# One joint key maximum for the first batch, an order of use for its loads, and weight splitting queued behind its attention on VectorE

## The chip, the cores and the metric

The kernel runs on one core of a Trainium2 chip. The metric is the time of one execution on the device in microseconds (us). The core's engines work in order, each on its own queue: PE multiplies matrices (PEld is its loading of weights), DVE is VectorE, ACT is ScalarE, POOL is GpSimd, and SP here only issues DMAs. They wait for one another through semaphores.

## The reference

Everything is float32; there are 8 batches, 8 heads, 576 rows and 64 columns per head (512 columns together).

```python
q_s = softmax(q, axis=-1)            # over the 64 columns of a row
k_s = softmax(k, axis=2)             # over the 576 rows: one maximum per column of k
kv  = einsum('bhsd,bhse->bhde', k_s, v)
x   = einsum('bhsd,bhde->bhse', q_s, kv)        # heads side by side: 576 x 512
xk, xr = mu_k*x + (1-mu_k)*x_prev, mu_r*x + (1-mu_r)*x_prev   # x_prev: one row earlier
y   = sigmoid(xr @ w_r) * (relu(xk @ w_k)**2 @ w_v)           # 512->512, 512->1024->512
u   = y + real(fft(fft(y, axis=1), axis=2))
out = u + relu(layernorm(u) @ w_ch1) @ w_ch2                  # 512->2048->512
```

q, k, v come in float32; the weight matrices come in 64 bits per element and are turned into float32 on the chip, by `split64`.

## The kernel before

There are three stages: attention with the first pair of matrix layers (until about 690 us), the transform, and the last pair of layers. The change is in the first stage, at its start.

**Attention of one batch n.** Work on k and v goes by head pairs hp = 0 to 3: `k_load` fetches a pair of heads of k and of v, `k_max` takes the maximum over five row blocks in VectorE, `k_col` transposes the 128x128 rest on TensorE (L188), takes one maximum per column (`kc`) and puts it on a diagonal (`kd`); `k_sub` multiplies the diagonal by a matrix of ones (L198), which spreads the maxima over all partitions, and subtracts them from k (L200); `k_exp` is ScalarE's exponential; `k_kv` multiplies with v in ten matrix instructions (L221); `k_out` divides and splits the product in a high and a low part (`kvh` by ScalarE, `kvl` by VectorE, L237). Work on q goes by three row groups T, B and L: `q_load`, `q_max`, `q_sub`, `q_exp`, `q_sum`, `q_mul` (GpSimd), `q_tr` (transposes, L330, and a split). `q_x` multiplies both and leaves x in `xb` (ScalarE's copies, L354 to L361).

**The matrix layers** go by blocks c = 0 to 11 of 384 rows; block 0 needs batch 0, block 1 needs batches 0 and 1, block 2 batch 1. `mix_diff` and `mix_part` make xk and xr (VectorE, with a high part by ScalarE and a low part by GpSimd), `m_wk` is xk @ w_k in eight slices f (L438 to L440), `m_r` is xr @ w_r, `m_wv` the product with w_v (L469 to L471).

**Weights.** Twenty pieces of 128x512 (eight of w_k, four of w_r, eight of w_v) go through five buffers `raw`. A piece is loaded by SP (L62), scaled by ScalarE (L67, L71), put together by VectorE in two steps (L72, L75), rounded to its high part by ScalarE (L81) and given a low part by GpSimd (L82), after which its buffer is free. The high and low parts of w_v lie where batch 0's attention and block 0's mixing had buffers (`spare`).

**What sets the order.** The framework plans the whole program at build and puts the instructions of each engine in a fixed order: the earliest in the text goes first among those that its own estimate has ready. So a later piece of text fills gaps of an earlier one. Buffers of one name (tag) are given out in the order of the text; PE's order in the trace is that of the `pa` tiles in the text. Attention's small matrix products and transposes share the four PSUM buffers `pa`, the column maxima `km` have two buffers, a k tile (`kt`) two, and q's exponentials (`qe`) one. Two waits are written by hand (`after`): the first five weight loads wait for the last load of batch 0 (`early[0]`), and all k and q loads of batch 1 wait for the high part of weight piece 5 (`early[1]`, L81). SP issues batch 0's loads as k pair 0, q T, B, L, then k pairs 1 to 3; GpSimd's queue issues v of pairs 0 and 1.

## Time and profile before

| | us |
|---|---|
| median of three runs (lowest, highest) | 1672.36 (1671.45, 1673.94) |
| the profiled execution | 1676.39 |
| its span, first to last instruction | 1674.6 |
| PE busy | 1548.0 (92%) |
| DVE, ACT, POOL busy | 746.7, 594.9, 491.5 |

The profile is of one execution. Its page gives each engine's busy time and cuts the span into 40 slices of 41.9 us; the views below list instructions in order of time, sums over stretches, and groups of equal instructions.

### The profile page before, as it was taken

The page shows a single profiled execution, that of the slowest core. Times are in us where ns is not written, and L with a number is a line of the kernel's source. Part 1 is how long each engine was busy: PE and PEld are TensorE (multiplying, and loading weights), DVE is VectorE, ACT ScalarE, POOL GpSimd, SP SyncE. Part 2 cuts the span into 40 slices and gives each one's busy share as a digit, 9 for nine tenths or more (in the row PEclk, how much of TensorE's full clock was granted, in tenths as well). Part 3 has the DMA queues.
Part 4 walks back from the last instruction along what each step waited for, and adds up shares of the span by engine and source line. Part 5 has one row for each costly group of instructions (what it writes and reads, how often), then busy time and mean ns, then how long its engine had stood idle before and what let it go on. Part 6 is the DMA issues. An engine that isn't in the chain of part 4 may idle for free.

```text
span 1674.6 us, 19835 instructions
## 1 busy us (share of the span) xinstructions
PE 1548.0 (92%) x7560; PEld 1313.2 (78%) x7560; DVE 746.7 (45%) x1342; ACT 594.9 (36%) x1120; POOL 491.5 (29%) x532
## 2 busy tenths in 40 slices
PE   2497999899989999987887999999999999999998
PEld 2476899788879888776765888888888888888886
DVE  7966544645365442199999312212221313131211
ACT  4673666566556564233445111111111111111110
POOL 4464663646365555265445000000000000000000
PEclk9598999999999999988999999999999999999999
DMA  7521322222212101435454101001010101010000
GB/s 196 164 83 51 85 56 68 64 56 70 69 51 63 58 13 51 170 110 196 167 192 157 51 0 41 11 1 50 1 51 1 50 1 51 0 51 1 26 0 26
DMA packets 117863, 108.91 MB, mean 65 GB/s; under 512 B 54760, under 2 KB 91752, under 8 KB 117512
## 3 DMA queue, kind: packets, MB, share of 16 engines
q1 hardware_dynamic: 107736, 84.37, 17.1%
q10 hardware_dynamic: 8064, 14.68, 2.4%
q0 software_dynamic: 1968, 8.60, 1.4%
q8 instruction: 59, 0.97, 0.2%
q14 instruction: 36, 0.29, 0.1%
HBM read 79.31 MB, written 28.31 MB: 64 GB/s over the span
## 4 chain that ended last, share of the span: by engine, by line
PE 66%; DVE 12%; issue 10%; POOL 4%; ACT 4%; DMA 3%; SPq 1%; POOLq 0%; ACTq 0%; DVEq 0%
PE ph L853 6%; PE ph L855 6%; PE pc L900 6%; PE ph L854 6%; PE pc L902 6%; PE pc L901 6%; PE pv L469 3%; PE pv L470 3%; PE pv L471 3%; PE pk L438 3%; PE pk L439 3%; PE pk L440 3%; DVE xm L416 2%; PE pr L454 1%; PE pr L455 1%
## 5 line engine op out<-in xcount | busy, mean ns | idle before, releaser
L859 DVE SCALAR_TENSOR_TENSOR hl<-ph,hh 128x512 fp32r<-128x512 f32 x144 | 99.2, 689 | 443.8 <-ACT hh L858 443.8
L858 ACT ACTIVATE hh<-ph 128x512 fp32r<-128x512 f32 x144 | 85.9, 597 | 515.3 <-PE ph L855 515.3
L884 POOL DMA_INDIRECT out_dram<-ua,rev x16 | 15.7, 979 | 732.0 <-DVE ua L905 731.6
L902 PE MATMUL pc<-w2h,hl 128*128 128x512 f32 x576 | 222.9, 393 | 8.2 <-DVE hl L859 8.2
L900 PE MATMUL pc<-w2h,hh 128*128 128x512 f32 x576 | 226.5, 393 | 3.9 <-ACT hh L858 3.9
L901 PE MATMUL pc<-w2l,hh 128*128 128x512 f32 x576 | 224.8, 390 | 0.0
L416 DVE SCALAR_TENSOR_TENSOR xm<-dt,omu,xb 128x63 f32<-128x63 f32 (+4 forms) x224 | 115.7, 566 | 83.2 <-POOL xr_lo L425 35.0
L438 PE MATMUL pk<-xk_hi,wk_hi 128*128 128x384 f32 x384 | 131.0, 350 | 12.4 <-ACT xk_hi L424 11.4
L446 POOL TENSOR_TENSOR kk_lo<-h,kk_hi 128x384 fp32r<-128x384 f32 x96 | 98.8, 1033 | 148.6 <-ACT h L445 130.7
L902 PEld LDWEIGHTS pc<-w2h,hl 128*128 128x128 f32 x576 | 107.6, 188 | 35.3 <-DVE hl L859 11.6
L439 PE MATMUL pk<-xk_lo,wk_hi 128*128 128x384 f32 x384 | 131.4, 343 | 0.2 <-POOL xk_lo L425 0.2
L900 PEld LDWEIGHTS pc<-w2h,hh 128*128 128x128 f32 x576 | 108.1, 188 | 29.9 <-ACT hh L858 6.5
L853 PE MATMUL ph<-uha,w1h 128*128 128x512 f32 x320 | 127.7, 401 | 2.8 <-ACT w1h L81 2.8
L440 PE MATMUL pk<-xk_hi,wk_lo 128*128 128x384 f32 x384 | 130.1, 340 | 0.0
L855 PE MATMUL ph<-uha,w1l 128*128 128x512 f32 x320 | 127.3, 398 | 1.2 <-POOL w1l L82 1.2
L854 PE MATMUL ph<-ula,w1h 128*128 128x512 f32 x320 | 126.8, 396 | 0.0
L901 PEld LDWEIGHTS pc<-w2l,hh 128*128 128x128 f32 x576 | 108.2, 188 | 23.6
L469 PE MATMUL pv<-wv,kk_hi 128*128 128x512 f32 x288 | 113.1, 394 | 0.6 <-ACT sgt L458 0.6
L470 PE MATMUL pv<-wv,kk_hi 128*128 128x512 f32 x288 | 112.9, 394 | 0.0
L471 PE MATMUL pv<-wv,kk_lo 128*128 128x512 f32 x288 | 112.4, 393 | 0.0
L853 PE MATMUL ph<-uhb,w1h 128*128 128x512 f32 x256 | 100.9, 397 | 0.0
L855 PE MATMUL ph<-uhb,w1l 128*128 128x512 f32 x256 | 100.0, 391 | 0.0
(206 smaller groups left out, 3178.6 us busy)
## 6 DMA issues: line engine op xcount, KB each, us to landing
raw<-in_moe_w_ch_dram SPq DMA_DIRECT2D x32, 512.0 KB
x1d<-sgt ACTq DMA_DIRECT2D x36, 256.0 KB
ua<-ud SPq DMA_DIRECT2D x36, 256.0 KB
kt<-in_k_dram SPq DMA_DIRECT2D x32, 256.0 KB
xtt<-x1d SPq DMA_DIRECT2D x8, 1024.0 KB
vt<-in_v_dram SPq DMA_DIRECT2D x60, 128.0 KB
qtT<-in_q_dram SPq DMA_DIRECT2D x8, 512.0 KB
qtB<-in_q_dram SPq DMA_DIRECT2D x8, 512.0 KB
```

Of the source, the lines that this page charges most:

```text
L438: nc.tensor.matmul(pk, wh, xk_hi[:, kt], start=kt == 0, stop=False)
L439: nc.tensor.matmul(pk, wh, xk_lo[:, kt], start=False, stop=False)
L440: mm = nc.tensor.matmul(pk, wl, xk_hi[:, kt], start=False, stop=kt == NK - 1)
L469: nc.tensor.matmul(pv, kk_hi[f][:, ts], wv_hi[f // 2][:, f % 2], start=f == 0, stop=False)
L470: nc.tensor.matmul(pv, kk_hi[f][:, ts], wv_lo[f // 2][:, f % 2], start=False, stop=False)
L471: mm = nc.tensor.matmul(pv, kk_lo[f][:, ts], wv_hi[f // 2][:, f % 2], start=False, stop=f == NF1 - 1)
L853: nc.tensor.matmul(ph_, w1h[f][:, kt], uh[:, kt], start=kt == 0, stop=False)
L854: nc.tensor.matmul(ph_, w1h[f][:, kt], ul[:, kt], start=False, stop=False)
L855: nc.tensor.matmul(ph_, w1l[f][:, kt], uh[:, kt], start=False, stop=kt == NK - 1)
L900: nc.tensor.matmul(a, hh[:, cs], w2h[f], start=f == 0, stop=False)
L901: nc.tensor.matmul(a, hh[:, cs], w2l[f], start=False, stop=False)
L902: nc.tensor.matmul(a, hl[:, cs], w2h[f], start=False, stop=f == NF2 - 1)
```

## The change

Batch 0's key work is regrouped. All four `k_load` are issued with one `q_load` after each of the pairs 1, 2 and 3; then all four `k_max`; then q group T's first steps; then one `k_cols`, which transposes the four maxima into one PSUM tile, takes all column maxima in one instruction, builds one diagonal tile of 128x512 and spreads it with one matrix product. The per-pair steps `k_shift`, `k_kv`, `k_out` follow, with q's steps between them. For the weights, the first of VectorE's two steps of each piece (`sign`, L72 of before) is ordered behind the last `kvl` and the last `q_tr` subtraction of batch 0; the order is one on VectorE's queue alone, with no semaphore. The second step depends on the first. The new diagonal tile takes 2 KB of a partition, and GpSimd's memory for DMA descriptors is set to 4096 bytes.

```diff
@@ -57,11 +57,16 @@
             ins.ins, to, mybir.DependencyInfo(mybir.DependencyClass.Sync, mybir.DependencyReason.DATA), reason="pace"
         )

+    def behind(ins, to):
+        tc.add_manual_dep(
+            ins.ins, to, mybir.DependencyInfo(mybir.DependencyClass.NoSync, mybir.DependencyReason.DATA), reason="order"
+        )
+
     def raw64(pool, dst, src, n, bufs, eng):
         raw = pool.tile([P, 2 * n], I32, tag="raw", name="raw", bufs=bufs)
         return raw, eng.dma_start(dst(raw), src)

-    def split64(raw, hi, lo, low_on_dve=False):
+    def split64(raw, hi, lo, low_on_dve=False, late=()):
         low, high = raw[:, 0::2], raw[:, 1::2]
         scaled = high.bitcast(F32)
         nc.scalar.activation(out=scaled, in_=scaled, func=AF.Copy, scale=2.0**-112)
@@ -69,9 +74,11 @@
             nc.vector.tensor_scalar(low, low, 29, None, op0=ALU.logical_shift_right)
         else:
             nc.scalar.activation(out=low, in_=low.bitcast(U32), func=AF.Copy, scale=LOW_SCALE, bias=LOW_BIAS)
-        nc.vector.scalar_tensor_tensor(
+        sign = nc.vector.scalar_tensor_tensor(
             out=low, in0=high, scalar=-(2**31), in1=low, op0=ALU.bitwise_and, op1=ALU.bitwise_or
         )
+        for to in late:
+            behind(sign, to)
         nc.vector.scalar_tensor_tensor(
             out=low, in0=high, scalar=3, in1=low, op0=ALU.logical_shift_left, op1=ALU.bitwise_or
         )
@@ -192,11 +199,33 @@
             nc.vector.tensor_scalar(kd, ident, kc, None, op0=ALU.mult)
             state["kd", n, hp] = (kd, pm)

+
+        def k_cols(pool):
+            pm, bm = (ps.tile([P, NHP, P], F32, tag="pa", name=f"p{i}m0", bufs=4) for i in "mb")
+            for hp in range(NHP):
+                nc.tensor.transpose(pm[:, hp], state.pop(("km", 0, hp)), ident)
+            kc = pool.tile([P, NHP], F32, name="kc4")
+            nc.vector.tensor_reduce(out=kc, in_=pm, axis=AX.X, op=ALU.max)
+            kd = pool.tile([P, NHP, P], F32, name="kd4")
+            nc.vector.tensor_tensor(
+                out=kd,
+                in0=ident.unsqueeze(1).to_broadcast([P, NHP, P]),
+                in1=kc.unsqueeze(2).to_broadcast([P, NHP, P]),
+                op=ALU.mult,
+            )
+            nc.tensor.matmul(bm.rearrange("p h n -> p (h n)"), ones, kd.rearrange("p h n -> p (h n)"), start=True, stop=True)
+            for hp in range(NHP):
+                state["bm", hp] = bm[:, hp]
+
         def k_sub(n, hp):
             kt = state["k", n, hp]
-            kd, pm = state.pop(("kd", n, hp))
-            nc.tensor.matmul(pm[:, P : 2 * P], ones, kd, start=True, stop=True)
-            ka = pm[:, P : 2 * P].rearrange("p (h d) -> p h d", h=2)
+            if n == 0:
+                ka = state.pop(("bm", hp))
+            else:
+                kd, pm = state.pop(("kd", n, hp))
+                ka = pm[:, P : 2 * P]
+                nc.tensor.matmul(ka, ones, kd, start=True, stop=True)
+            ka = ka.rearrange("p (h d) -> p h d", h=2)
             nc.vector.tensor_tensor(
                 out=kt, in0=kt, in1=ka.unsqueeze(2).to_broadcast([P, 2, 5, DH]), op=ALU.subtract
             )
@@ -234,7 +263,7 @@
                 )
             for h in range(2):
                 r = slice(h * DH, (h + 1) * DH)
-                nc.vector.scalar_tensor_tensor(
+                ins = nc.vector.scalar_tensor_tensor(
                     out=kvl[0][r, hp, r],
                     in0=pk[r, r],
                     scalar=rs[r],
@@ -242,6 +271,8 @@
                     op0=ALU.mult,
                     op1=ALU.subtract,
                 )
+                if n == 0:
+                    last["k"] = ins.ins.name

         def q_load(n, g):
             if g == "L":
@@ -336,7 +367,9 @@
                     cs = slice(j, w, 2) if g == "T" else slice(w - 1 - j, None, -2)
                     o = (qh[:, :, cs], ql[:, :, cs], qh.bitcast(F32)[:, :, cs])
                 nc.scalar.copy(o[0], ptv)
-                nc.vector.tensor_tensor(out=o[1], in0=ptv, in1=o[2], op=ALU.subtract)
+                ins = nc.vector.tensor_tensor(out=o[1], in0=ptv, in1=o[2], op=ALU.subtract)
+                if n == 0:
+                    last["q"] = ins.ins.name
             state["qT", n, g] = (qh, ql, w)

         def q_x(n, g):
@@ -363,6 +396,8 @@

         done = set()

+        last = {}
+
         KST = [k_load, None, k_max, k_col, k_shift, k_kv, k_out]
         QST = [q_load, None, None, q_max, q_sub, q_exp, q_sum, q_mul, q_tr, q_x]

@@ -490,7 +525,7 @@
             if src is w_v:
                 hi, lo, i = hi[i // 2], lo[i // 2], i % 2
             at = (slice(None), slice(None), cs) if by_col else (slice(None), i)
-            return split64(raw, hi[at], lo[at])
+            return split64(raw, hi[at], lo[at], late=last.values())

         NRAW = 5
         pieces = [(w_k, wk_hi, wk_lo, f, True) for f in range(NF1)]
@@ -530,13 +565,22 @@

         with tc.tile_pool(name="wst", bufs=1) as wst:
             for hp in range(NHP):
-                for i, fn in enumerate((k_load, k_max, k_col, k_shift, k_kv, k_out)):
+                k_load(0, hp)
+                if hp:
+                    q_load(0, "TBL"[hp - 1])
+            for hp in range(NHP):
+                k_max(0, hp)
+            for fn in (q_max, q_sub, q_exp):
+                fn(0, "T")
+            k_cols(wst)
+            for hp in range(NHP):
+                for fn in (k_shift, k_kv, k_out):
                     fn(0, hp)
-                    if i == 0 and hp == 0:
-                        for g in "TBL":
-                            q_load(0, g)
+                if hp < 2:
+                    for fn in (q_max, q_sub, q_exp):
+                        fn(0, "BL"[hp])
                 if hp < 3:
-                    for fn in (q_max, q_sub, q_exp, q_sum, q_mul, q_tr):
+                    for fn in (q_sum, q_mul, q_tr):
                         fn(0, "TBL"[hp])
             for g in "LTB":
                 q_x(0, g)
@@ -975,7 +1019,7 @@
     from concourse import mybir as _mybir
     from concourse.bass_utils import run_bass_kernel_spmd as _run

-    nc = _bacc.Bacc("TRN2", target_bir_lowering=False, num_devices=1)
+    nc = _bacc.Bacc("TRN2", target_bir_lowering=False, num_devices=1, dynamic_dma_scratch_size=4096)
     arrays, args = {}, []
     tab_s, tab_d = _tables()
     for name, a in [(n, inputs[n]) for n in _INS] + [("tab_s", tab_s), ("tab_d", tab_d)]:
```

## Rows read from the trace of the kernel before

**Rows 1.** The page's forty slices of the span: PE's busy tenths.
```profile
PE   2497999899989999987887999999999999999998
```

**Rows 2.** Windows of the start: length; PE, PEld, DVE, ACT, POOL busy (count); PE clock.
```profile
0.00:20.00 20.00, 3.78 (x13) 2.92 (x13) 12.67 (x29) 4.67 (x5) 6.07 (x16) 1.00 0.78 179
20.00:43.00 23.00, 7.03 (x30) 6.10 (x30) 21.47 (x33) 14.27 (x28) 12.59 (x8) 0.96 0.72 215
43.00:73.00 30.00, 15.62 (x63) 13.52 (x63) 29.08 (x47) 21.77 (x40) 9.96 (x7) 0.50 0.72 218
73.00:96.00 23.00, 16.00 (x75) 14.65 (x76) 19.20 (x33) 13.65 (x31) 17.73 (x19) 0.73 0.32 94
96.00:126.00 30.00, 26.79 (x139) 22.90 (x138) 16.23 (x29) 22.48 (x39) 14.70 (x13) 1.00 0.17 43
126.00:154.00 28.00, 21.15 (x109) 18.40 (x108) 13.42 (x29) 8.14 (x19) 8.50 (x13) 0.76 0.17 51
```

**Rows 3.** Instructions in order of time on PE: start, length, line [idle before].
```profile
25.89 0.42 PE L188 MATMUL pm<-ident,km 128*128 128x128 f32 x1
...
73.64 0.41 PE L188 MATMUL pm<-ident,km 128*128 128x128 f32 x1
80.18 1.01 PE L438 MATMUL pk<-xk_hi,wk_hi 128*128 128x384 f32 x2 [6.12 <-ACT xk_hi L424]
...
127.24 1.28 PE L221 MATMUL pkv<-vt,ek 128*128 128x130 f32 x10
...
136.04 0.39 PE L471 MATMUL pv<-wv,kk_lo 128*128 128x512 f32 x1
```

**Rows 4.** Instructions in order of time on ACT, first 170 us.
```profile
42.93 0.66 ACT L81 CAST wk_hi<-raw 128x512 fp32r<-128x512 f32 x1 [1.06 <-DVE raw L75]
...
154.09 0.59 ACT L359 COPY xb<-pxB 128x512 f32<-128x512 f32 x1 [0.29 <-PE pxB L352]
```

**Rows 5.** Instructions in order of time on DVE, first 90 us.
```profile
22.91 0.58 DVE L237 SCALAR_TENSOR_TENSOR kvl<-pkv,rs,kvh 64x64 fp32r<-64x64 f32 x2 [0.51 <-ACT kvh L232]
...
28.37 0.69 DVE L72 SCALAR_TENSOR_TENSOR raw<-raw 128x512 int32<-128x512 int32 x1
...
36.00 1.79 DVE L72 SCALAR_TENSOR_TENSOR raw<-raw 128x512 int32<-128x512 int32 x1
...
89.17 1.35 DVE L179 TENSOR_REDUCE km<-kt 128x128 f32<-128x640 f32 x1
```

**Rows 6.** Windows again, of the weights' `raw` tiles alone: DVE, ACT, POOL.
```profile
43.00:73.00 30.00, 15.72 (x18) 17.48 (x29) 9.96 (x7) 0.50 0.72 218
...
sum 180.00, DVE 37.26 ACT 36.42 POOL 29.97; mean DVE 5.32 ACT 5.20 POOL 4.28
```

**Rows 7.** DMA issues on SP in order of time.
```profile
84.11 0.39 SPq L158 DMA_DIRECT2D kt<-in_k_dram  x1
```

**Rows 8.** The chain that ended last, at its start.
```profile
5.03 9.40 DMA ql<-in_q_dram
```

**Rows 9.** Groups of DVE and PE in the first 80 us: count, busy us, mean ns.
```profile
L200 DVE TENSOR_TENSOR kt<-kt,pm 128x640 f32<-128x640 f32 x4 | 3.2, 812 | 0.0
L264 DVE TENSOR_REDUCE qmL<-ql 64x8 f32<-64x512 f32 x2 | 1.3, 674 | 0.4 <-DMA ql<-in_q_dram 0.4
L221 PE MATMUL pkv<-vt,ek 128*128 128x130 f32 x40 | 10.1, 440 | 14.9 <-ACT ek L207 14.9
L198 PE MATMUL pm<-kd,ones 128*128 128x128 f32 x8 | 3.2, 502 | 13.6 <-DVE kd L192 8.0 <-DMA raw<-in_moe_w_k_dram 5.6
L330 PE MATMUL ptT<-ident,qeT 128*128 128x128 f32 x8 | 2.0, 428 | 6.5 <-POOL qeT L303 6.5
```

**Rows 10.** Instructions in order of time on POOL.
```profile
35.86 6.49 POOL L82 TENSOR_TENSOR wk_lo<-raw,wk_hi 128x512 fp32r<-128x512 f32 x4 [2.14 <-ACT wk_hi L81]
...
107.59 1.31 POOL L82 TENSOR_TENSOR wv<-raw,wv 128x512 fp32r<-128x512 f32 x1 [1.84 <-ACT wv L81]
```

**Rows 11.** DMA issues by line over the whole span: size, us to landing.
```profile
vt<-in_v_dram POOLq DMA_DIRECT2D x4, 128.0 KB, 7.5
```

## The prediction

> **What bounds the kernel now.** I read the page's slices first. PE is busy nearly throughout, except in the first two slices of 41.9 us (2 and 4 tenths) and the fourth (7 tenths) [rows 1]. A change in batch 0 can only be worth what PE idles there. The windows of the start come next [rows 2]: between 20 and 73 us DVE is busy 50.6 of 53 us while PE has 22.7 of 53, at the lower of its two clock levels (granted 0.50, 1.2 GHz) from 43 on. From 96 us on DVE is no longer full (16.2 of 30), PE is (26.8 of 30); then comes a second hole, 126 to 154 us, where PE has 21.2 of 28 us and DVE, ACT and POOL are all below half. So there are two different limits: VectorE first, then a chain of waits.
>
> The time view of PE shows the chain's stations [rows 3]. Head pair 1 of batch 0 starts its column transpose at 25.89; batch 0's q_x ends and batch 1's first transpose (L188) follows at 73.64; block 0's first m_wk starts at 80.18 and its last m_wv ends at 136.43; batch 1's last k_kv starts at 127.24; ScalarE's last copy of batch 1's x ends at 154.09 + 0.59 = 154.7 [rows 4]. Block 1 needs that copy. PE's second hole is the wait for batch 1, and its chain, 73.64 to 154.7 = 81.0 us, starts where batch 0 ends. That is the number that matters: **what the change is worth is how much earlier batch 1's x is complete**, not how much earlier block 0 starts.
>
> **The change part by part.** *Loads.* The 3.54 MB of q, k and v (three times 8 x 576 x 64 x 4 bytes) at 179 GB/s [rows 2] take 19.8 us in either order. With k pair 3 and its v in front of q L only, its k lands at about 18.5 us. The L load took 9.4 us and the chain ran through it [rows 8]; at the end of the list nothing but the weights' loads stands behind it. If it takes as long there, these start at about 31 us instead of right behind the rest, and five of them (0.52 MB each) at 179 GB/s are in by 46, the first by 34; cover: VectorE takes the first up at about 42 (below) and needs over 1 us for each. Without that cover it would cost the difference, up to 9 us.
>
> *Joint maximum.* Before, the pairs went one after another: four times transpose, kc, kd, L198, k_sub. Now: last k_max to 19.8 us, transposes to 20.2; then two operations of 128x512 that the trace does not have. For the reduction and the diagonal I take 0.68 us each, from the 64x512 reduction [rows 9] (bounds: 0.3, not better than the same work on a quarter; 1.4, all lanes twice as slow); 21.6 us. The product with ones over 512 columns lies between 0.8 us, what the two passes over 128 columns took in all (3.2 / 4) [rows 9], and four times that, 3.2; I take 2.2, since columns and not the start make up most of it; 23.8. The first k_sub 0.81 [rows 9] and an exponential of about the same length: the first k_kv at 25.4. Four of them take 10.1 us and the three transposes of q lying between them 2.0 + 2.0 + about 1 [rows 9] (the last two bounded by the first): 40.5. k_out's parts are near 0.6 each (two instructions 0.58) [rows 5], with a ScalarE part of that kind ahead of them: 42 us, with 38 and 48 as bounds. The rest of q_x, three of each twelve products, about 3 us: 45, against 73.6. Block 0's first m_wk follows q_x by 80.18 - 73.64 = 6.5 us: 51.5 instead of 80.2.
>
> *Weights behind attention.* VectorE's two steps now cannot begin before 42 us; they began at 28.37 [rows 5]. Nothing is saved: in all the weights hold VectorE 37.3 us in this stage [rows 6], and they move as a block from beside batch 0 to beside block 0's mixing and batch 1. What queues behind: ScalarE's L81, then GpSimd's L82, and since the five buffers are freed by L82 only, SP stands at the sixth weight load, with batch 1's loads behind it. And batch 1's loads wait by hand for piece 5's L81. In the trace that came at 42.93 + 0.66 = 43.6, 15.2 us after the first L72. Now five pieces lie scaled in their buffers when VectorE comes, so the way from first L72 to piece 5's L81 is between one piece's round (two steps of 0.69, L81 0.66, L82 1.3, a load of 0.52 MB / 179 GB/s = 2.9, scaling by two ScalarE instructions at about 36.4 / 60 = 0.6 [rows 6], two steps and L81 again: 9.5) and 15.2; I take 12.5: 54.5. **This is the step that goes the wrong way**: batch 1's loads come 11 us later than before. From SP's issue to the end of k_max were 89.17 + 1.35 - 84.11 = 6.4 us for a later pair [rows 5, 7], so batch 1's first transpose comes at 61, not at 73.64: 12.6 us earlier. Before, its k had lain ready and waited for q_x.
>
> *Batch 1's chain.* I keep its 81 us: 142 instead of 154.7. Bounds: its four head pairs took 127.24 - 73.64 = 53.6 us, 13 per pair; the links beside a free PE could be some 3 us shorter each (down to 69 us in all), and some 12 longer if weights lie in its way.
>
> *Is anything else late by then?* Block 0 took 136.4 - 80.2 = 56.3 us on PE; from 51.5 it would end at 108, and its second half needs w_v, whose last low part ended at 107.59 + 1.31 = 108.9 [rows 10], 27.5 us before block 0's end. What VectorE did beside weights from 43 to 73 us, 29.1 - 15.7 = 13.4 us [rows 2, 6], I take for batch 1's maxima, and as much again for mixing: w_v is through at 42 + 37.3 + 26.8 = 106 us and block 0 at about 134. Batch 1's 142 hides it with 8 us to spare. VectorE's whole work from 20 to 154 us was 99.4 us [rows 2]; without the 22 us at most that belong to batch 0 up to 42, 77 remain for the 100 us to 142: it fits, without much room.
>
> *The smaller descriptor memory.* GpSimd issues six v loads at the start (landing after 7.5 us [rows 11]), three tables and sixteen row scatters, far apart. If it had to wait for room at the start, v pairs 0 and 1 would come up to 7.5 us later, at about 14 to 20 us; the first k_kv at 25.4 covers that. I take 0.
>
> **Sum.** The profiled execution took 1676.4 us, 1.8 more than its span; 12.6 us less is 1663.8. It lies 4.0 us above the median of the runs shown, so for the median 1672.36 - 12.6, rounded, **1660 us**. After block 1 the rest is PE-bound and moves along.
>
> **A rule against it.** GpSimd's low parts and VectorE's steps collide: an L72 takes 0.69 us alone and 1.79 us beside a run of L82 (four in 6.49 us) [rows 5, 10]. The Trainium skill, page "SBUF — State Buffer", section "Who interferes with whom", says that a VectorE instruction with two SBUF inputs and a GpSimd instruction that reads SBUF exclude each other for the whole instruction. The trace agrees for these two lines; by the rule a piece would cost VectorE and GpSimd together the sum of their steps, and packing them behind attention would cost more than the measured sum of VectorE. It is the third rival, priced from rows.
>
> **The rivals.** *First, a larger gain (0.22):* batch 1's chain shortens as well. For: PE has nothing dense to do from block 0's end on, and the pairs' links before waited behind its matrix products. Against: most links wait for VectorE or ScalarE, and one buffer `qe` makes q's part serial. Priced with its bound of 69 us the x of batch 1 is ready at 130 us, 24.7 us earlier: 1648.
>
> *Second, no change (0.13):* batch 1's chain loses what its start gains. Its k chain has about twenty VectorE steps; if each waits once for a weight step of mean 37.3 / 40 = 0.93 us, with a third of these waits known from before, it grows by some 12 us: 1672. For: VectorE has hardly any gap from 42 to 106 us. Against: the second half of that chain ran with VectorE at half, and weights are over by then.
>
> *Third, slower (0.16):* the weights become late, and block 0 with them. If VectorE's and GpSimd's work exclude each other, the twenty pieces take 40 x 0.69 + 30.0 [rows 5, 6] = 57.6 us, with the 26.8 as before: w_v at 126.4 and block 0's end at 154. Before, block 0 was through at 136.4 and PE stood 28 - 21.2 = 6.8 us in the second hole; of the 17.6 us of delay 10.8 are then lost: 1683. It decides from where block 0 ends after 136.4 + 6.8 = 143. For: the 1.79 us above, and PE at its lower clock while it is fed piece by piece. Against: the mean over all steps is 0.93, not 1.79 us, and attention's own VectorE steps can run beside L82.
>
> That the change does not do what it says, the order on VectorE being there already, is excluded: the first L72 at 28.37 comes right behind pair 1's transpose at 25.89 [rows 3, 5], two pairs before the last `kvl`.
>
> **How the numbers follow.** Forecast 0.46, larger gain 0.22, none 0.13, slower 0.16; the remaining 0.03 is for other orders of the plan. 0.2% is 3.3 us, about what a measurement can tell from no change. Of the forecast's own spread (gain 5 to 20 us, 1652 to 1667 us) nearly all is faster, so faster 0.70, within 0.2% 0.13, slower 0.17. For 8 in 10 the range takes in most of the larger gain and the unchanged case and the beginning of the slower: 1645 to 1677.
>
> **What would show it.** In the changed kernel: one 512-column product at about 22 us; no L72 before about 42; block 0's first m_wk near 51; piece 5's L81 at 52 to 58; batch 1's first L188 at 58 to 65; its last x copy near 142 with PE waiting for it. The forecast is wrong if PE's second hole is gone while block 0 is still running (third rival), or if batch 1's first transpose is early but its x is not (second).

## The result and the profile after

The changed kernel takes **1682.06 us** in the median (1681.35 to 1683.89, 4 runs) against 1673.15 us (1671.45 to 1674.31, 4 runs) before: ratio 1.0056, 95% interval 1.0038 to 1.0073. It is slower by about 9 us; 1660 was forecast. The profiled execution took 1681.35 us (span 1679.5); the profiled one of the kernel before lies 3 us above its median here.

The first views are those of [rows 1] and [rows 2]: PE's busy tenths in the page's slices, then the windows of the start (length; PE, PEld, DVE, ACT, POOL busy with counts; PE clock), of the changed kernel.

```profile
PE   3458999899989999978788999999999999999998
```
```profile
0.00:20.00 20.00, 1.39 (x3) 0.54 (x3) 10.48 (x24) 2.34 (x2) 7.44 (x17) 1.00 0.80 184
20.00:43.00 23.00, 14.97 (x87) 12.69 (x87) 18.20 (x38) 15.72 (x31) 3.46 (x3) 1.00 0.47 141
43.00:73.00 30.00, 9.45 (x40) 7.72 (x40) 29.12 (x33) 17.29 (x35) 24.05 (x20) 0.72 0.53 163
73.00:96.00 23.00, 21.09 (x107) 19.10 (x106) 22.97 (x31) 16.12 (x32) 13.40 (x11) 0.92 0.55 169
96.00:126.00 30.00, 12.12 (x40) 9.38 (x39) 23.08 (x37) 19.09 (x36) 15.56 (x12) 0.57 0.32 94
126.00:154.00 28.00, 22.98 (x116) 19.42 (x116) 9.62 (x18) 7.60 (x15) 5.49 (x4) 0.93 0.17 51
```

PE gained 8 us between 20 and 43, batch 0's attention, and lost 14.7 between 96 and 126, where it had been nearly full and now has 12.1 of 30 us. It stands there for 6.64 us, until 103.4 us, for one diagonal (`kd`, shown further below); its granted clock, 0.92 in the window before, is 0.57 in the mean. VectorE did less before 43 us (28.7 against 34.1 us) and more from 73 to 126 (46.1 against 35.4).

The stations that answer to [rows 3 to 5, 10], in order of time on PE, ACT, DVE and POOL of the changed kernel (start, length, line):

```profile
26.42 2.08 PE L216 MATMUL pbm<-kd,ones 128*128 128x512 f32 x2 [3.11 <-DVE kd L210]
...
58.30 1.01 PE L473 MATMUL pk<-xk_hi,wk_hi 128*128 128x384 f32 x2 [13.56 <-ACT xk_hi L459]
...
72.34 0.45 PE L195 MATMUL pm<-ident,km 128*128 128x128 f32 x1 [5.32 <-DVE km L186]
...
133.71 1.28 PE L250 MATMUL pkv<-vt,ek 128*128 128x130 f32 x10
...
145.48 0.39 PE L506 MATMUL pv<-wv,kk_lo 128*128 128x512 f32 x1
```
```profile
60.82 0.70 ACT L88 CAST wk_hi<-raw 128x512 fp32r<-128x512 f32 x1
...
163.47 0.58 ACT L392 COPY xb<-pxB 128x512 f32<-128x512 f32 x1
```
```profile
42.79 0.69 DVE L77 SCALAR_TENSOR_TENSOR raw<-raw 128x512 int32<-128x512 int32 x1
```
```profile
117.52 1.29 POOL L89 TENSOR_TENSOR wv<-raw,wv 128x512 fp32r<-128x512 f32 x1 [3.26 <-ACT wv L88]
```

Block 0 starts 21.9 us earlier than before (58.30 against 80.18) and ends 9.4 us later; the last weight piece is done at 118.8 instead of 108.9; batch 1's x is complete at 163.47 + 0.58 = 164.05 instead of 154.68. Block 11, the end of the first stage (read where VectorE takes up its last product), follows at 715.6 instead of 708.4. Two times matter from here on: **x1**, at which batch 1's x is complete, and what follows x1.

### The profile page after: what moved, and what is told of

Its sections match the earlier page's. It is cut to its first block, busy times and chain, and to the rows that moved or that the text cites. A ratio compares the mean times of both kernels' runs of the same rounds, so it can differ in the third digit from the quotient of the medians.

```text
span 1679.5 us, 19809 instructions
## 1 busy us (share of the span) xinstructions
PE 1547.0 (92%) x7554; PEld 1311.0 (78%) x7554; DVE 754.8 (45%) x1336; ACT 592.4 (35%) x1118; POOL 499.2 (30%) x532
## 4 chain that ended last, share of the span: by engine, by line
PE 70%; DVE 10%; issue 9%; POOL 3%; ACT 2%; DMA 2%; POOLq 0%; ACTq 0%; SPq 0%; DVEq 0%
PE ph L897 7%; PE ph L899 6%; PE pc L946 6%; PE ph L898 6%; PE pc L944 6%; PE pc L945 6%; PE pv L504 4%; PE pv L505 4%; PE pv L506 4%; PE pk L473 3%; PE pk L474 3%; PE pk L475 3%; PE pr L489 2%; PE pr L490 2%; PE pr L491 2%
## 5 line engine op out<-in xcount | busy, mean ns | idle before, releaser
L473 PE MATMUL pk<-xk_hi,wk_hi 128*128 128x384 f32 x384 | 130.0, 347 | 20.1 <-ACT xk_hi L459 18.2
```

What stands on the lines that cost most here:

```text
L473: nc.tensor.matmul(pk, wh, xk_hi[:, kt], start=kt == 0, stop=False)
```

## The experiments

All runs were timed against the kernel before on the same chip. The table has a profiled execution of each (us; "weights" is the last low part of w_v; "rest" is the span less x1; "590 to 660" is PE's busy time in that window, whose length is 70 us). A row of the table is one execution, while the times of one kernel in one series lie several us apart (17 of the kernel before: 1672.6 to 1678.1). So small differences of "rest" mean nothing by themselves; the ratio, from all runs, decides.

| kernel | first weight step | weights | x1 | block 11's end | 590 to 660 | rest | ratio (95% interval) |
|---|---|---|---|---|---|---|---|
| before | 28.4 | 108.9 | 154.7 | 708.4 | 70.0 | 1519.9 | 1 |
| after | 42.8 | 118.8 | 164.1 | 715.6 | 70.0 | 1515.5 | 1.0056 (1.0038, 1.0073) |
| e1 no order | 27.0 | 110.5 | 149.4 | 706.3 | 65.6 | 1527.7 | 1.0031 (1.0019, 1.0042) |
| e2 gate at piece 2 | 42.3 | 114.9 | 157.6 | 716.0 | 66.0 | 1529.6 | 1.0094 (1.0079, 1.0110) |
| e3 own room | 42.1 | 118.2 | 157.5 | 711.6 | 65.7 | 1531.8 | 1.0102 (1.0086, 1.0117) |
| e4 low parts zero | 42.0 | – | 146.9 | 707.0 | 65.9 | 1527.8 | 1.0002 (0.9993, 1.0011) |
| e5 small memory alone | 28.6 | 109.4 | 154.6 | 707.7 | 70.0 | 1519.1 | 0.9998 (0.9989, 1.0007) |
| e6 loads alone | 29.2 | 110.5 | 155.0 | 709.7 | 65.6 | 1521.1 | 1.0037 (1.0024, 1.0050) |
| e7 joint maximum | 25.9 | 104.7 | 153.3 | 708.2 | 65.6 | 1529.0 | 1.0066 (1.0054, 1.0078) |
| e8 order alone | 51.9 | 128.9 | 171.5 | 727.3 | 65.6 | 1527.3 | 1.0178 (1.0165, 1.0192) |
| e9 first 8 free | 27.2 | 112.8 | 154.3 | 706.5 | 70.0 | 1515.8 | 0.9997 (0.9987, 1.0007) |
| e10 first 2 free | 25.5 | 114.8 | 162.8 | 715.9 | 70.0 | 1519.2 | 1.0066 (1.0052, 1.0080) |
| e11 no order, gate 6 | 26.7 | 107.5 | 148.5 | 706.7 | 66.0 | 1524.0 | 1.0000 (0.9991, 1.0008) |
| e12 behind pair 0 | 35.1 | 114.8 | 158.1 | 716.4 | 65.9 | 1523.9 | 1.0060 (1.0047, 1.0073) |
| e13 first 10 free | 26.5 | 108.7 | 151.8 | 702.3 | 70.0 | 1515.0 | 0.9987 (0.9978, 0.9996) |
| e14 first 8 free, gate 7 | 26.7 | 110.8 | 156.6 | 708.8 | 70.0 | 1516.4 | 1.0019 (1.0008, 1.0030) |
| e15 first 10 free, gate 6 | 26.8 | 111.4 | 155.0 | 714.3 | 66.0 | 1526.8 | 1.0062 (1.0049, 1.0075) |

**e1_no_order: the order taken away.**

```diff
-            return split64(raw, hi[at], lo[at], late=last.values())
+            return split64(raw, hi[at], lo[at])
```

> The changed kernel without the order of the weights behind attention on VectorE; joint maximum and order of loads stay. Theory A (the weights, moved as a block, end later: the last low part of w_v at 118.8 instead of 108.9 us, and block 0 and batch 1's chain end 9.4 us later with it): weight steps fill VectorE's gaps between 7 and 42 us again, w_v ends at 100 to 109 us, time 1660 to 1674 us. Rival B (the joint maximum or the new order of loads itself costs the time): still 1678 to 1683 us, with w_v's end at most a little earlier.

x1 is 14.7 us earlier than after, and even 5.3 earlier than before; block 11 ends 9.3 us earlier than after. So the order on VectorE is what delays the first stage, though the weights' end (110.5) lies 1.5 us beyond theory A's range. The time, 1680.94 us, is rival B's all the same: what follows x1 grew by 12 us against after (1527.7 to 1515.5). That needed experiments of its own (e9 on).

**e2_gate_piece2: batch 1's loads released by weight piece 2 instead of 5.**

```diff
-                if i == 5:
+                if i == 2:
                     early[1] = ins.ins.name
```

> The changed kernel, but batch 1's loads wait for the high part of weight piece 2 instead of piece 5 (about 52 instead of 61.5 us). Theory A (the end of w_v sets block 0's end and holds batch 1's chain): w_v's end stays at 117 to 122 us, block 0's end at 145 to 149, time 1679 to 1685 us. Rival C (the later loads of batch 1 set its chain): batch 1's first transpose and its x come some 9 us earlier, time 1671 to 1675 us.

Batch 1's first key load is issued at 52.1 instead of 61.6 and its first transpose runs at 64.1 instead of 72.3, but its last k_kv only at 130.3 (133.7): of 8.2 us at the transpose 6.4 are left at x1, none at block 11's end (the window 590 to 660 alone takes 4 us back). Neither side's figures hold: the weights end 2 us before theory A's range and block 0 at 140.2 (145 to 149 expected), and the time is above both ranges. So the forecast's step that goes the wrong way is real, and by x1 the earlier gate wins back most of the 9.4 us; but it moved the weights' end too, so this run does not separate the two.

**e3_own_room: `sgt` and one more pair of block 0's buffers in memory of their own instead of the weights' room.**

```diff
-        NK0 = 4
+        NK0 = 5
+        sgt = [p1.tile([P, D], F32, name=f"sgt{i}") for i in range(3)]
...
-        sgt = [pl.tile([P, D], F32, name=f"sgt{i}") for i in range(3)]
```

> The changed kernel with the three sigmoid buffers and the fifth pair of kk buffers in memory of their own, no longer in the room of the weights' raw buffers. Theory A in the form that block 0's m_r, and batch 1's last pair queued behind it on PE, wait for the room of the last raw buffers: m_r and batch 1's fourth maximum product run some 8 us earlier (119 instead of 127 us), batch 1's x 4 to 8 us earlier, time 1674 to 1678 us. Theory A in the form that only w_v itself is late, and rival C: no change, 1680 to 1684 us.

The rows of e3 on POOL and PE: the weights are no earlier (113.84 + 4.31 = 118.2), yet block 0's last product runs 11.4 us earlier than after.

```profile
113.84 4.31 POOL L89 TENSOR_TENSOR wv<-raw,wv 128x512 fp32r<-128x512 f32 x3 [3.42 <-ACT wv L88]
```
```profile
134.07 0.40 PE L507 MATMUL pv<-wv,kk_lo 128*128 128x512 f32 x1
```

So block 0's second half hung on the release of the weights' buffers: m_r (`pr`), which waits for `sgt`, starts at 103.50 instead of 121.74. Batch 1's last product with ones, expected 8 us earlier, comes 2.1 us earlier (124.93, 127.03). x1 gains 6.6 us, as expected; what follows loses 16, so the time is 1691.98 us where 1674 to 1678 was expected.

**e4_low_memset: GpSimd writes zeros for the weights' low parts and leaves the subtraction out.**

```diff
-        nc.gpsimd.tensor_tensor(out=lo, in0=wf, in1=hi.bitcast(F32), op=ALU.subtract)
+        if late:
+            nc.gpsimd.memset(lo.bitcast(F32), 0.0)
+        else:
+            nc.gpsimd.tensor_tensor(out=lo, in0=wf, in1=hi.bitcast(F32), op=ALU.subtract)
```

> The changed kernel, leaving out the low parts of the twenty weight pieces: GpSimd sets them to zero with an instruction that reads nothing. If VectorE's weight steps are long because they exclude each other with GpSimd's subtractions (36.2 us for 40 steps, 0.9 each, against 0.69 alone), they fall to 27 to 30 us in all, w_v ends at 104 to 112 us and the time is 1667 to 1675 us. If not, they stay at 36 us, w_v's end moves by at most the shorter GpSimd step of the last piece, and the time is 1679 to 1683 us.

The windows of the weights' tiles (DVE, ACT, POOL) in e4, and the kd step that is 3.48 us long in the changed kernel (further below):

```profile
sum 98.00, DVE 29.78 ACT 34.50 POOL 0.00; mean DVE 7.44 ACT 8.63 POOL 0.00
```
```profile
92.59 0.26 DVE L202 TENSOR_SCALAR kd<-ident,kc 128x128 f32<-128x128 f32 x1
```

VectorE's weight steps take 29.8 us instead of 36.2, as the theory has it, and x1 comes 17.2 us earlier. But the edit does more than take the subtraction's reads away. The zeros wait for no weight: GpSimd writes those of w_k and w_r at 6.65 to 12.3 us and those of w_v by 46.5, long before most pieces are split, and a piece's buffer is free as soon as ScalarE has rounded it. So the 17.2 us hold the collision of the two engines, GpSimd's missing work and the earlier release of the buffers, and are not a price of the collision.

**e5_scratch_only, e6_loads_only, e7_joint_only, e8_order_only: the parts one by one.** e5 sets the descriptor memory in the kernel before; e6 only reorders its loads; e7 has the joint maximum and its order of steps (and the small memory, which it needs for its diagonal) with the old loads and no order; e8 adds only the order.

```diff
 e5 (before):  num_devices=1)  ->  num_devices=1, dynamic_dma_scratch_size=4096)
 e6 (before):
+for hp in range(NHP):
+    k_load(0, hp)
+    if hp:
+        q_load(0, "TBL"[hp - 1])
 for hp in range(NHP):
-    for i, fn in enumerate((k_load, k_max, k_col, k_shift, k_kv, k_out)):
+    for fn in (k_max, k_col, k_shift, k_kv, k_out):
...
 e7 (after, without the order):
                 k_load(0, hp)
-                if hp:
-                    q_load(0, "TBL"[hp - 1])
+                if hp == 0:
+                    for g in "TBL":
+                        q_load(0, g)
 e8 (before):
-            return split64(raw, hi[at], lo[at])
+            return split64(raw, hi[at], lo[at], late=last.values())
...
```

> The kernel before with the smaller descriptor memory alone. Theory (priced at 0 in the prediction): ratio 1.000 within 0.001, block 11's end at 708.4 us within 0.5, and the stretch from the first product of stage 2 to the first of stage 3 stays 121.9 us. Rival: the smaller memory moves tiles and with them the order written out for stages 2 and 3, and this is where the run without the order lost its lead (its stretch there was 126.0 us): then the stretch grows by 3 to 5 us and the ratio is 1.002 to 1.003.

> The kernel before with the new order of the loads alone, four k and v loads first with q between them. Theory: pair 1's chain no longer stands behind the slow q load, VectorE and the weights have nothing new in their way; batch 0's four k_kv come up to 5 us earlier, block 11's end 705 to 708, ratio 0.998 to 1.000. Rival: the weights' first loads stand behind the slow q load and VectorE starves between 20 and 40 us: first weight step after 32 instead of 28.4, block 11's end 711 to 714, ratio 1.002 to 1.004.

> The joint key maximum and its order of steps with the old order of the loads, weights free. Theory (the joint maximum alone is worth little, since all four pairs now wait for the last of them): the four k_kv start at 35 to 40 us, block 11's end 706 to 710, ratio 1.000 to 1.003. Rival: it was the loads that held the run without the order back, and the joint maximum gains alone: block 11's end below 703, ratio under 0.999.

> The kernel before with VectorE's order alone: the weights stand behind the last kvl and the last q low part of batch 0, which goes pair after pair as before. Theory (the order is what costs, by the time at which the weights begin and VectorE idles before): batch 0's chain alone ends at about 48 to 52 us, so the weights begin 6 to 9 us later than in the changed kernel, whose end of w_v moves from 118.8 to 125 to 128; block 11's end 721 to 725, 1687 to 1692 us, ratio 1.007 to 1.010. Rival (the joint maximum costs and the order is neutral): block 11's end 706 to 710, ratio 0.999 to 1.002.

The small memory does nothing, as priced (every instruction stands where it did, and the time is the same; block 11's end, 707.7, is 0.2 us below the range). e8 goes the way of its theory, with sizes above every range: weights from 51.9, x1 17 us late, the time 29 us longer (some 12 of them after x1). e6 has its rival's ratio without its mechanism (the weights begin at 29.2, not after 32), and e7 the expected end of block 11 with a ratio far above. Their x1 is that of before or 1.4 us earlier, so neither the loads nor the joint maximum delays batch 1, and yet the kernels are 6 and 11 us slower. The row of e8 on DVE:

```profile
51.91 1.29 DVE L77 SCALAR_TENSOR_TENSOR raw<-raw 128x512 int32<-128x512 int32 x2
```

**e9_first8_free, e10_first2_free: the order for a part of the weights.** The first 8 (2) of 20 pieces may run beside attention.

```diff
-            return split64(raw, hi[at], lo[at], late=last.values())
+            return split64(raw, hi[at], lo[at], late=last.values() if npc[0] > 8 else ())
...
+                npc[0] = i + 1
```

> The changed kernel with the first 8 of the 20 weight pieces free to run beside batch 0's attention, the other 12 ordered behind it. The order written out for VectorE, TensorE and ScalarE from stage 2 on is the same as before's, instruction by instruction. Theory (VectorE's idle time before 42 us is what the order cost, and stages 2 and 3 lose time of their own wherever their written order differs from before's): first weight step near 27, w_v's end 106 to 111, block 11's end 703 to 709 us, from the first product of stage 2 to the first of stage 3 122 us within 1, ratio 0.996 to 1.001. Rival (the joint maximum with the new loads costs by itself, and the later stages merely follow block 11's end): ratio 1.002 to 1.004 as without any order.

> The changed kernel with the first 2 weight pieces free and 18 ordered; from stage 2 on the written order is before's. Theory: two pieces less behind 42 us, some 3.6 us of VectorE and GpSimd (2 x 1.8) earlier: w_v's end near 115, block 11's end 711 to 713, the stretch of stage 2 122 us within 1, ratio 1.002 to 1.004. Rival: as the changed kernel (block 11's end 715 to 716, ratio 1.0056) if the length of the weights is set by collisions with GpSimd and not by when they begin.

With 8 free pieces the whole loss is gone (x1 154.3, ratio 0.9997), though the weights end 1.8 us later than expected and the stretch of stage 2 took 119.2 us, shorter than expected. With 2 the weights end 4 us earlier, as expected, but x1 gains 1.3 us and the time nothing: the rival. PE waited 8.06 us for one kd there (6.64 in the changed kernel), and the third head pair loses more: its exponential comes after `sgt` on ScalarE and its k_kv after m_r on PE, at 124.58 (116.36 in the changed kernel).

**e11_free_gate6, e12_behind_pair0.** e11 is e1 with the gate one piece later; e12 orders the weights behind pair 0's `kvl` alone.

```diff
 e11 (e1):
-                if i == 5:
+                if i == 6:
 e12 (after):
-                if n == 0:
+                if n == 0 and hp == 0:
                     last["k"] = ins.ins.name
...
-                    last["q"] = ins.ins.name
+                    pass
```

> All weights free (no order on VectorE), with batch 1's loads gated by the seventh weight piece instead of the sixth; from stage 2 on the written order is that of the changed kernel (which took 121.5 us for the stretch), not that of the run without the order (126.0 us). Theory (the written order of stages 2 and 3 sets its length): block 11's end 705 to 708 us, the stretch 121 to 123 us, ratio 0.999 to 1.001. Rival (the stretch follows from something in stage 1 that the missing order brings): the stretch stays at 126 us and the ratio at 1.002 to 1.004.

> The weights ordered behind the kvl of head pair 0 alone (at about 33 us in the changed kernel) instead of behind the last kvl and the last q low part. From stage 2 on the written order is that of the changed kernel. Theory (when the weights begin decides): first weight step at 32 to 34, w_v's end 110 to 114, block 11's end 707 to 711, stretch 121 to 123, ratio 1.000 to 1.003. Rival (attention that weights no longer stand in front of is worth as much as the weights' delay): block 11's end 704 to 706, ratio under 0.999.

e11's ratio is 1.0000 as expected, but not by the stretch named: that was 124.5 us, and after block 11 the whole took 965.8 us (e1 970.8, before 966.2). e12 missed: the first weight step (35.1) and the end of the weights (114.8) are about 1 us outside what was expected, block 11's end (716.4) is 5 us beyond it. Against e9 it is 10 us late there, 3.8 of them in x1 and 4 in the window 590 to 660; where the other 2 arise is open.

**e13_first10_free, e14_first8_gate7, e15_first10_gate6: the later order of instructions held, and one part of it not.** When a variant changes the first 150 us, the plan made at build writes other orders for later parts of the program too. Comparing the instruction lists position by position: in e5, e9, e10, e13 and e14 TensorE and VectorE have before's order in the last part of the first stage and in all that follows; after differs in 75 of TensorE's 4248 records behind block 11. In e15 TensorE's order differs in most of the last 1500 positions of the first stage, and neither TensorE's nor VectorE's from stage 2 on.

```diff
 e13 (e9): npc[0] > 8   ->  npc[0] > 10
 e14 (e9): if i == 5:   ->  if i == 7:
 e15 (e13): if i == 5:  ->  if i == 6:
```

> The changed kernel with the first 10 weight pieces free, 10 ordered. The written order of TensorE and VectorE is before's, instruction by instruction, in the last part of stage 1 and from stage 2 on. Theory (the later stages depend on the written order alone, so the time is that at which batch 1's x is complete plus 1515 to 1520 us): x complete at 149 to 154 us as with 8 pieces free or without the order, ratio 0.996 to 1.000. Rival (the later stages lose time in every kernel with the joint maximum): ratio 1.002 or more.

> The first 8 weight pieces free and batch 1's loads gated by the eighth piece; written order of the later parts as before's. Theory: x of batch 1 complete at 149 to 155 us, the time that plus 1515 to 1520, ratio 0.996 to 1.000; whether the later gate helps (as it seemed to without the order: x at 148.5 instead of 149.4 us) shows in x alone. Rival (the gate decides when batch 1 is ready): x later than 156 us, ratio 1.002.

> The first 10 weight pieces free and batch 1's loads gated by the seventh piece; the written order is before's from stage 2 on, but not in the last part of stage 1 (893 of TensorE's last 1500 instructions there stand elsewhere). Theory (that part of the written order costs by itself): from the completion of batch 1's x to block 11's end 556 to 560 us instead of 552 to 554, the rest after block 11 as before's 964 to 967 us. Rival (it costs nothing): 552 to 554 us there too.

**e13 is the only kernel here that is faster than before, by 2.2 us**: 1671.40 us against 1673.62 on its chip, 0.9987 (0.9978 to 0.9996). e14 is its rival as far as batch 1 goes (the later gate puts x1 at 156.6, ratio 1.0019), while the rest is 1516.4 as the theory has it. e15 has the hole and the delay that the theory says: 559.3 us from x1 to block 11's end. PE between 590 and 660 us in e13, then in e15, and the longest idle time in e15's hole:

```profile
590.00:660.00 70.00, 70.00 (x367) 1.00 0.08 25
```
```profile
590.00:660.00 70.00, 65.98 (x342) 1.00 0.03 12
```
```profile
637.26 0.61 PE L474 MATMUL pk<-xk_hi,wk_hi 128*128 128x384 f32 x2 [1.23 <-ACT xk_hi L460]
```

The column 590 to 660 of the table separates the kernels without exception: 70.0 where the later order is before's (or after's), with a rest of 1515.0 to 1519.9 us; 65.6 to 66.0 where it is another, with a rest of 1521.1 to 1531.8. There PE stands about 4 us for mixing (`xk_hi`, `xr_hi`), for which it has no wait there in the good order. The rest separates them by 1.2 us only, less than two executions of one kernel can differ. The other part of the longer rest lies in the later stages, where e1, e2, e3, e7 and e8 take 970.8 to 977.8 us after block 11 and all others at most 967.7. Which instruction there costs it was not traced, and the order alone does not settle it: e1 and e7 have the same order on TensorE, VectorE and ScalarE after block 11 and take 970.8 and 974.1 us there, and e6, whose order differs from before's in 380 TensorE positions, takes 966.4 (before 966.2).

## Why the prediction was wrong

**Right: when the weights begin, in part by luck.** The diagonal, the column maxima and the product took 0.68, 0.67 and 2.08 us (0.68, 0.68 and 2.2 estimated), the last `kvl` came at 42.2 and the first weight step at 42.79 (42). But the joint product began at 26.42, 4.8 us after the forecast's 21.6, because the last `k_max` ended at 22.8 instead of 19.8 and steps of q went between; the first k_kv came at 30.34 (25.4 forecast), and four k_kv with their transposes then took 9.9 us instead of 15.1, at a granted clock of 1.00. The two errors cancel. Block 0's first m_wk came at 58.30 (51.5): after the last product of q_x, 44.7, PE stood 13.56 us for `xk_hi`, where 6.5 was forecast. By x1 the loads (e6) and the small memory (e5) cost nothing.

**Wrong: "is anything else late by then?"** This is the step that failed first. The prediction had w_v through at 106 us. Its term 26.8, VectorE's other work beside the weights, was the 13.4 us of one window taken twice. The windows of the weights' tiles in the changed kernel (DVE, ACT, POOL):

```profile
43.00:73.00 30.00, 16.41 (x19) 12.44 (x21) 13.33 (x9) 0.72 0.53 163
73.00:96.00 23.00, 7.77 (x10) 8.78 (x15) 4.41 (x4) 0.92 0.55 169
96.00:126.00 30.00, 11.79 (x13) 9.78 (x16) 10.61 (x8) 0.57 0.32 94
```

From the first weight step to the end of the last (42.79 to 116.75 us) VectorE was busy 72.9 of 74.0 us: 36.2 for weights, 36.7 for other work. ScalarE's and GpSimd's steps of the last piece add 2 us. (By the three windows, which reach to 126, it is 29.12 + 22.97 + 23.08 = 75.2 us, 36.0 of them for weights and 39.2 for other work.) The kernel before told as much, in two rows of the same view that the prediction did not take:

```profile
73.00:96.00 23.00, 3.22 (x5) 4.33 (x7) 6.94 (x5) 0.73 0.32 94
96.00:126.00 30.00, 5.45 (x6) 4.35 (x7) 5.29 (x4) 1.00 0.17 43
```

With [rows 2, 6] that is 13.4 + (19.20 - 3.22) + (16.23 - 5.45) = 40.1 us, and 42 + 37.3 + 40.1 = 119 us, near where the weights ended (118.8); that it is so near is partly luck, since this sum reaches to 126 us and leaves the last piece's 2 us out. VectorE's idle time before 42 us, which weights had filled, never comes back.

**Wrong: "Batch 1's 142 hides it", that is, that block 0 and batch 1 run beside each other.** The forecast carried the 27.5 us from w_v's end to block 0's end along (106 to 134), and they held: 118.8 to 145.9, 27.1 us. What it left out is that batch 1 hangs on the same end. The chain of waits in the changed kernel (start, length, what):

```profile
116.06 0.70 DVE raw L82
116.77 0.02 issue
116.79 0.66 ACT wv L88
117.45 0.07 issue
117.52 1.30 POOL wv L89
118.82 0.02 issue
118.84 0.94 ACT kk_hi L479 x2
...
121.09 0.61 ACT sgt L493
121.70 0.04 issue
121.74 0.80 PE pr L489
...
127.23 0.43 PE pm L227 x2
```

`kk_hi` and `sgt` lie where the weights' buffers were, so ScalarE writes them as soon as GpSimd has read the last piece, and PE's m_r (L489) waits for `sgt`. Behind m_r in PE's queue stands batch 1's last head pair (L227). Its diagonal on DVE and its product on PE, before and then in the changed kernel:

```profile
119.45 0.29 DVE L192 TENSOR_SCALAR kd<-ident,kc 128x128 f32<-128x128 f32 x1
120.78 0.39 PE L198 MATMUL pm<-kd,ones 128*128 128x128 f32 x2
```
```profile
121.14 0.29 DVE L199 TENSOR_SCALAR kd<-ident,kc 128x128 f32<-128x128 f32 x1
127.03 0.63 PE L227 MATMUL pm<-kd,ones 128*128 128x128 f32 x2
```

The diagonal is 1.7 us late, the product 6.2: it waits behind m_r. The weights, block 0 and batch 1 moved by 9.4 to 9.9 us together. e3, which loosened the link, wins back 6.6 of x1's 9.4 us with the weights hardly earlier (118.2). The weights' end is not all of it, though: in e2, e10 and e12 it lies at 114.8 to 114.9 us, and x1 at 157.6, 162.8 and 158.1.

**Wrong: batch 1's first transpose at 61.** It came at 72.34, 1.3 us before that of the kernel before. From the first weight step to the end of piece 5's L88 (L81 of before) it took 18.7 us (42.79 to 61.52), outside the stated 9.5 to 15.2: VectorE's mixing steps (L440, two runs of 2.94 and 2.67 us) stand between weight steps, and piece 5, whose load was issued at 49.5, is taken up by ScalarE at 56.6 only. And from SP's issue of the first key load (61.55) to the end of the first `k_max` 10.6 us, not 6.4. So the early start, the whole gain of the forecast, did not come.

**Wrong: "I keep its 81 us".** Batch 1's chain took 72.34 to 164.05, 91.7 us. Its third k_kv starts at 116.36, only 1.8 us later than before (114.58), so 3.1 of the 10.7 us of growth lie up to there and the other 7.6 behind it, where the last pair waits for m_r. One short step in it is long, on DVE, beside GpSimd (POOL), in the changed kernel:

```profile
99.22 0.67 DVE L82 SCALAR_TENSOR_TENSOR raw<-raw 128x512 int32<-128x512 int32 x1
99.82 0.14 DVE L258 RECIPROCAL rs<-rs 128x1 f32<-128x1 f32 x1
99.89 3.48 DVE L199 TENSOR_SCALAR kd<-ident,kc 128x128 f32<-128x128 f32 x1
103.29 0.68 DVE L82 SCALAR_TENSOR_TENSOR raw<-raw 128x512 int32<-128x512 int32 x1
```
```profile
98.03 2.77 POOL L334 TENSOR_TENSOR qeL<-qeL,qsL 64x512 f32<-64x512 f32 x1
100.76 2.53 POOL L89 TENSOR_TENSOR wv<-raw,wv 128x512 fp32r<-128x512 f32 x2
```

kd takes 3.48 us and ends 0.1 us after GpSimd's run of instructions; PE waits 6.64 us for it. It takes 0.26 us in e4 and 0.26 and 0.29 us for the next two pairs of the changed kernel, all at times when GpSimd stood idle. The Trainium skill, page "SBUF — State Buffer", section "Who interferes with whom", says that VectorE and GpSimd share one pair of ports under an exclusive lock, and that `tensor_scalar` can take the pair. The trace agrees: 3.48 us beside GpSimd, 0.26 to 0.29 without it; e10 has a kd of 4.72 us that ends with a run of GpSimd too. Before, weights met this as well (37.3 us in all, 36.2 after), and one of batch 1's four kd took 0.66 us. But this wait is not what made the kernel slower: the second k_kv is 8 us late (106.48 against 98.53), the third only 1.8, and e9 and e13, which lose nothing in time, have a wait for kd of 8.02 and 7.93 us.

**The third rival comes nearest, and its price fits by luck** (1683 against 1682.06). Right are its direction, weights and block 0 late, and its point of decision: block 0 ends at 145.9, after 143. But it put w_v's end at 126.4 by letting all weight steps exclude each other, and the steps did not grow; and by its own rule, that block 0 fills PE's second hole of 6.8 us, an end at 145.9 costs 2.7 us, some 1675. The hole was not filled: from block 0's end to x1 there are 18.2 us, as before, and all of it moved. The second rival has the chain's growth right (10.7 us, 12 forecast), but no early start to set against it. **The first, and the second as a forecast of no change, are excluded** by x1, 9.4 us later, and by the ratio.

**Not in the prediction at all:** that the later order of instructions changes with the start. In the changed kernel it hardly did, but the rest of the undone and partial variants grew by up to 16 us, some 4 of them in the window 590 to 660 with another order, which hid what the parts are worth. By x1 alone the joint maximum with its loads and free weights is worth 5.3 us (e1) or 6.2 (e11); e13, with the better order later, has 2.9 of it, and 2.2 us in the median time. Also, of the 9 us that the median shows the two profiled executions have 5 (1681.35 against 1676.39, which lay above its median): the rest, 4.4 us shorter after the change by the table, may be no more than the spread of executions.

Open: why e12, with weights from 35.1 us, has x1 at 158.1 while e9, from 27.2, has 154.3 with weights that end 2 us apart; what lengthens the stages after block 11 in e3 and e7; why batch 1's first keys took 10.6 us from issue to maximum; and the 2.8 us by which e3's x1 is still later than before's.

## What to carry to other kernels

Work that is moved off a full engine's early gaps must be paid later: count that engine's other work over the whole stretch up to the new end, from the same windows, not from one of them. Two chains hide each other only if no queue and no buffer joins them: here the last step of one stood in PE's queue behind a product of the other, which waited for room that the weights held. Where a planner lays out the program, an edit at the start can rewrite the order of distant parts: compare the instruction order and the time after the edited part before an experiment's verdict is put down to the edit, and set differences of single traces against the spread of runs.

## What the runs showed of the hardware

A VectorE instruction (kd) of 0.26 to 0.29 us with GpSimd idle lasted 3.48 us beside three GpSimd instructions of 5.3 us in all, and ended 0.1 us after them. Two programs with the same order of instructions (before and e5) had block 11's end at 708.4 and 707.7 us and spans of 1674.6 and 1673.7 us in their profiled executions; yet 17 executions of the kernel before lay between 1672.6 and 1678.1 us, so one such pair does not show how far two executions can differ. TensorE's granted clock was 0.81 in the mean from 96 to 103 us of the changed kernel, of which it stood idle for over 6 us, and 0.50 from 103 to 126 us, its lower level (1.2 of 2.4 GHz); before, it was 1.00 from 96 to 126 us, with 26.8 of 30 us of work [rows 2].
